# Replayed instruction orders for attention and the second convolution, a LayerNorm by pairs, and one chunk transposed on TensorE

## The chip, the cores and the metric

The kernel runs on one core of one Trainium2 chip. A core has five engines that work at the same time, each through its own instructions in program order: TensorE (PE: matrix products; its weight loads are listed apart as PEld), VectorE (DVE: elementwise work), ScalarE (ACT: activation functions and copies), GpSimd (POOL) and SyncE (SP, which here issues the DMA transfers). They meet through semaphores. An instruction that has to wait holds up everything behind it on its own engine, so the order in which a program hands work to an engine is part of its speed. Operands lie in SBUF (128 partitions) and matrix products land in PSUM, from where ACT or DVE copies them out ("evacuates" them).

The metric is the device time of one execution in microseconds (us); less is better. Besides, one execution was recorded by the hardware profiler; all rows below come from that one.

## What is computed

Four residual layers on x of shape (1, 2048, 512) in bfloat16, each behind a LayerNorm: a long convolution (an S4 layer by FFT), a sliding-window attention, and both once more with the same weights.

```python
def _A_ref(u, A_re, ..., Dskip):                 # convolution
    K = jnp.einsum("dn,dnl,dn->dl", Cc, P, dB).real        # P = exp(dt * A * l)
    ...
    Yf = Uf * Kf[None, :, :, :]                  # spectra of u and K, both padded to 2L
    y = irfft2(Yf)[..., :L]
    return y + u * Dskip

def _B_ref(x, wqkv, wo):                         # attention: 32 heads of 16, window 8, dilation 2
    ...
    idx = pos[:, None] - (jnp.arange(8) * 2)[None, :]
    ...
    logits = jnp.einsum("bhsd,bhswd->bhsw", q, kg) * scale
    attn = _softmax(jnp.where(mask, logits, -1e9))
    o = jnp.einsum("bhsw,bhswd->bhsd", attn, vg)
    return o.transpose(0, 2, 1, 3).reshape(B, S, D) @ wo

x = A_u
x = x + _A_ref(_layernorm(x), ...)
x = x + _B_ref(_layernorm(x), ...)
x = x + _A_ref(_layernorm(x), ...)
x = x + _B_ref(_layernorm(x), ...)
```

## The kernel before

The 2048 positions lie as 128 partitions by 16 token columns j; a group q is four of these columns (q = 0 is j 0 to 3, q = 3 is j 12 to 15). The residual x stays in SBUF as the tile `X` from start to end. The program has four stages, one after the other in the trace.

Stage 1 (`kernel_and_first_conv`, 0 to about 237 us) makes the spectrum of the convolution's kernel and runs the first convolution, in an order written out by hand. Stage 2 is attention 1 (`b_layer`, about 237 to 369 us), stage 3 convolution 2 (`a_layer`, 369 to 440 us), stage 4 attention 2 (`b_layer` again, 440 to 575 us).

An attention goes through these steps. `start(q)` (lines 1062 to 1098) normalises a group of `X` into `xn` (statistics on DVE, the root on ACT, line 160, scaling on DVE, lines 177 to 181) and transposes it into `xnT`: groups 0 and 3 on PE with a copy by ACT (`pt_x` line 1086, copy line 1089), groups 1 and 2 by DMA. `proj` (line 1110) makes queries and keys in 32 groups of four matmuls, each copied out by ACT into `qT` or `kT` (line 1115). The 32 heads are two family pairs, fp = 0 and 1, with a tile each: `kT_4078` and `kT_4079` are those of fp 0 and 1 in attention 1 and `kT_6218` and `kT_6219` in attention 2; `L_4082` and `L_4083` are the logits of fp 0 and 1 in attention 1. `values` (line 1130) makes v, copied out into `VX` (line 1135). `logits(fp, half)` multiplies q by shifted k on DVE, one product of 128x2048 for each of the 8 window offsets (line 1161; for the first half of fp 0 it is cut into 16 of 128x1024), and sums over the head's 16 elements on PE with a block matrix of ones (`Lp`, line 1171). ACT copies the sums (`LT`, line 1186), PE turns them (`pt_l`), ACT copies them into `L` (line 1197), and GpSimd masks the edge (line 1230). `softmax` (lines 1216 to 1243) runs on DVE with the exponential on ACT. `pv(fp, j0, nj)`, below "PV", multiplies `VX` by the weights on DVE, again a product for each offset (line 1254), and PE sums the 8 products with an identity matrix into `po` (lines 1270 and 1275). ACT copies `po` out (lines 1290 and 1292), a DMA transposes it into `oT`, and `out(qt)` (lines 1322 and 1324, `ps_o` and `ps_w`) adds the output projection to `X`, copied back by ACT (lines 1409, 1411 and 1452). PV comes in the pieces PV(0,0), PV(1,0) (columns j 0 to 7 of a family pair), PV(0,8), and PV(1,8), PV(1,12), PV(1,14) with 4, 2 and 2 columns; the products of these are 128x2048, 128x1024 and 128x512.

Behind attention 1 `normed` (lines 1413 to 1447) makes the LayerNorm for convolution 2 by groups: for q = 0 to 2 the mean from sums that ACT gathered (`ln_nm`, DVE, line 1437), four squares on ACT (line 1426), a root on ACT (line 168), scale on DVE, and the normalised columns on ACT (line 1430) or DVE into `U`. For q = 3 the statistics are DVE's (line 147).

Convolution 2 goes through four chunks dc of 128 channels. `s1` (line 804) takes one group of four columns of `U` through a transform on PE; ACT casts it into `Z` (line 808). `turn` transposes a chunk's `Z` into four tiles `zt` by SP's DMA queue (line 819). `s2` (lines 829 to 832) makes `xp`, ACT casts it to `xc` (line 836), `product` multiplies by the spectrum on DVE (`pa`, `pb`, lines 846 to 849), `inverse` transforms back on PE (`vp`), half of it copied by ACT and half by DVE (`VT`, line 868), and `final` adds to `X`.

What sets the order in stages 2 to 4 is a planner, the class `Plan`. The layer functions don't issue instructions at once: they register operations with `op` (engine, a cost in us from a table of estimates, the function that issues, its predecessors, and the PSUM and SBUF buffers that it takes and drops). `run` lists them: `ranks` gives each a priority, `place` simulates five engines and picks by rank, and 1200 random changes of the ranks are tried with a fixed seed; the best order is then issued. Each layer is planned by itself, as if all its inputs were there at its start; a pseudo operation `late` in `a_layer` holds back group 3 of `U` by 5 us.

## Time and profile before

| | us |
|---|---|
| median of 3 runs | 577.17 (574.05 to 578.47) |
| profiled execution, its own time | 576.7 |
| its span, first to last instruction | 574.9 |
| stage 2, attention 1 | about 237 to 369 |
| stage 3, convolution 2 | about 369 to 440 |
| stage 4, attention 2 | about 440 to 575 |

Around the span lie 1.8 us (576.7 - 574.9). A row of the timeline has a start, the time to its end, engine, line and operation, the output and the inputs, how often it repeats without a gap, and, in square brackets, how long the engine had been idle just before and on what the wait ended. Instructions of one engine overlap a little, so the time from start to start is often shorter than the duration. A row of windows has, for one stretch of the span, its length, and the busy time of each engine with its number of instructions, the clock that was granted to PE (1.00 is full), and what the DMA engines did.

### The profile page before, as it was taken

How to read it: one execution, taken by the hardware profiler on the slowest of the kernel's cores; microseconds unless marked ns; L12 is line 12 of the kernel's file. 1: busy time of each engine (PE TensorE's matmuls, PEld its weight loads, DVE VectorE, ACT ScalarE, POOL GpSimd, SP SyncE). 2: the span in 40 equal slices, each digit the busy share in tenths (PEclk: the TensorE clock that was granted, in tenths of full speed). 3: DMA queues.
4: the chain of work that ended last, by engine and by line, in shares of the span. 5: the costliest groups of instructions: out<-in, count | busy, mean ns of one | idle time of the engine just before them, and what ended most of it. 6: DMA issues, size and time to landing. Idle time of an engine off the chain costs nothing. (4 is left out here: it accounts for less than half of the span.)

```text
span 574.9 us, 11556 instructions
## 1 busy us (share of the span) xinstructions
PE 414.5 (72%) x4806; PEld 234.9 (41%) x4806; DVE 477.6 (83%) x803; ACT 340.2 (59%) x509; POOL 12.9 (2%) x62
## 2 busy tenths in 40 slices
PE   1102466777586589799995788678976999965997
PEld 0101333363363466443562334355654434632353
DVE  5999999999799886949789996508999378999980
ACT  4999655354455468675752147988763656622234
POOL 0000000000000004000000000000000000000000
PEclk9999987697798899999997699989996899987999
DMA  8200363646545465231033025439200310031142
GB/s 278 96 1 0 48 124 90 94 111 130 92 112 112 83 167 188 84 67 41 15 92 73 1 40 153 192 70 183 44 2 3 71 41 15 29 100 38 37 92 110
DMA packets 96031, 47.69 MB, mean 83 GB/s; under 512 B 85106, under 2 KB 91250, under 8 KB 94698
## 3 DMA queue, kind: packets, MB, share of 16 engines
q1 hardware_dynamic: 94394, 46.55, 34.1%
q8 instruction: 37, 0.61, 0.4%
q10 hardware_dynamic: 1584, 0.39, 0.3%
q14 instruction: 16, 0.13, 0.1%
HBM read 15.77 MB, written 8.13 MB: 42 GB/s over the span
## 5 line engine op out<-in xcount | busy, mean ns | idle before, releaser
L1161 DVE TENSOR_TENSOR prod<-qT,kT 128x2048 bf16<-128x2048 bf16 (+1 forms) x80 | 75.6, 1006 | 19.0 <-ACT kT L1115 10.8
L1254 DVE TENSOR_TENSOR prod<-VX,L 128x2048 bf16<-128x2048 bf16 (+2 forms) x96 | 76.9, 863 | 5.5 <-PE po L1275 2.0
L1110 PE MATMUL ps_qk<-xnT,wqk 128*128 128x512 bf16 x256 | 63.1, 385 | 2.2 <-ACT qT L1115 2.0
L1270 PE MATMUL po<-prod,sb_ident 128*128 128x512 bf16 x224 | 57.8, 409 | 7.6 <-DVE prod L1254 6.1
L212 PE MATMUL psA<-X,sb_F 128*128 128x128 bf16 x128 | 12.2, 238 | 43.3 <-ACT X L637 33.2
L212 PEld LDWEIGHTS <-sb_F 128*128 128x128 bf16 x256 | 17.5, 107 | 56.8 <-issue 56.1
L1171 PE MATMUL Lp<-prod,sb_bones 128*32 128x512 bf16 x256 | 29.6, 415 | 14.1 <-DVE prod L1161 14.0
L1270 PEld LDWEIGHTS <-sb_ident 128*128 128x128 bf16 x224 | 23.1, 104 | 39.2 <-issue 16.2
L1110 PEld LDWEIGHTS <-wqk 128*128 128x128 bf16 x256 | 23.0, 99 | 33.4 <-issue 12.7
L1290 ACT CAST ot<-po 128x1024 bf16<-128x1024 f32 x14 | 13.6, 1016 | 35.8 <-PE po L1270 34.2
L1130 PE MATMUL ps_v<-wv,xnT 128*128 128x256 bf16 x256 | 33.2, 278 | 1.1 <-ACT xnT L1089 0.8
L606 ACT CAST KTq<-psk 128x1024 bf16<-128x1024 f32 (+1 forms) x9 | 8.3, 917 | 43.1 <-PE psA L237 41.2
L596 PE MATMUL psk<-Ttab 128*32 128x64 bf16 x1024 | 20.9, 199 | 16.3 <-issue 16.3
L215 ACT CAST Z<-psA 128x1024 bf16<-128x1024 f32 (+1 forms) x32 | 28.8, 973 | 4.7 <-PE psA L212 4.6
L1324 PE MATMUL ps_o<-wo_t,oT 128*128 128x512 bf16 x112 | 29.1, 379 | 0.0
L578 DVE TENSOR_TENSOR Ttab<-Ttab,MPA 128x2048 bf16<-128x2048 bf16 (+2 forms) x20 | 27.7, 1431 | 0.0
L1130 PEld LDWEIGHTS <-xnT 128*128 128x128 bf16 x256 | 23.7, 99 | 9.5 <-issue 4.8
L1135 ACT CAST VX<-ps_v 128x512 bf16<-128x512 f32 x32 | 18.6, 588 | 14.8 <-PE ps_v L1130 14.8
L578 DVE TENSOR_TENSOR Y2tab<-Ttab,MPB 128x6144 bf16<-128x6144 bf16 (+1 forms) x13 | 27.2, 2119 | 0.0
L1115 ACT CAST kT<-ps_qk 128x512 bf16<-128x512 f32 x32 | 18.8, 587 | 13.6 <-PE ps_qk L1110 13.3
L1115 ACT CAST qT<-ps_qk 128x512 bf16<-128x512 f32 x32 | 18.7, 588 | 13.1 <-PE ps_qk L1110 12.9
L309 ACT CAST VT<-psA 128x512 bf16<-128x512 f32 x32 | 17.2, 589 | 13.3 <-PE psA L275 12.2
(200 smaller groups left out, 1014.9 us busy)
## 6 DMA issues: line engine op xcount, KB each, us to landing
X<-in_A_u_dram SPq DMA_DIRECT2D x8, 512.0 KB, 5.3
kt_scratch<-Kt SPq DMA_DIRECT2D x4, 1024.0 KB, 5.1
Kt<-kt_scratch SPq DMA_DIRECT2D x4, 1024.0 KB, 8.9
out_dram<-X SPq DMA_DIRECT2D x4, 512.0 KB, 2.6
k_scratch<-KTq SPq DMA_DIRECT2D x7, 256.0 KB, 2.4
KT<-k_scratch SPq DMA_DIRECT2D x7, 256.0 KB, 2.8
VX<-VX SPq DMA_DIRECT2D x4, 448.0 KB, 4.5
kT<-kT SPq DMA_DIRECT2D x8, 192.0 KB, 2.2
```

The lines of the kernel that those rows point to most:

```text
L212: nc.tensor.matmul(o, F1[:, j, r, :], rhs_j(j), start=True, stop=not dk)
L215: nc.scalar.copy(Z[:, 0:n // 8, :, jq * 32:(jq + 1) * 32].rearrange("p g r k -> p r g k"), ps[:, :, 0:n // 8, :])
L578: nc.vector.tensor_tensor(dst, src.to_broadcast([128, q, n, 2 * EYB]), mm.to_broadcast([128, q * n, EYB, 2]), ALU.mult)
L596: nc.tensor.matmul(o.rearrange("e (s i) -> e s i", s=2), xs, T[:, 1:3, h, m // 2, :, t], start=(m == 0), stop=False, skip_group_check=True)
L1110: nc.tensor.matmul(ps[:], wqk[:, ct, f0:f0 + 128], xnT[:, 4 * s:4 * s + 4, ct, :], start=(ct == 0), stop=(ct == 3))
L1115: nc.scalar.copy((qT, kT)[which][fp][:, f2, o:o + 512], box.pop(("qk", which, fp, f2, s))[:])
L1130: nc.tensor.matmul(ps[:, jj].rearrange("p t h d -> p (t h d)"), xnT[:, j + jj, ct, :], wv[:, ct, fp * 256:(fp + 1) * 256], start=(ct == 0) ...
L1161: nc.vector.tensor_tensor(pr[:, 0:n2], qT[fp][:, a:a + n2, j0 * 128:j0 * 128 + 1024], kT[fp][:, a:a + n2, c0:c0 + 1024], ALU.mult)
L1171: nc.tensor.matmul(Lp[r0:r0 + 32, w // 4, :], bones[:, w % 4, :], pr[:, f2 - a, hb * 512:(hb + 1) * 512], start=(n == 1), stop=(n == 4), s ...
L1254: nc.vector.tensor_tensor(p2[:, 0:nj].rearrange("p j t d h -> p (j t) d h"), VX[:, fp, NV + a:NV + a + nj].rearrange("p j (t d h) -> p (j ...
L1270: nc.tensor.matmul(po[:, c:c + 512], ident[:], p2[:, k + j:k + j + 2].rearrange("p j t d h -> p (j t d h)"), start=(n == 1), stop=(n == W))
L1324: nc.tensor.matmul(ps, box["oT"][:, ft // 2, j, ft % 2, :], wo_t[:, ft, :], start=False, stop=(ft == 3))
```

## The change

Stage 1 stays as it was. In stages 2 to 4 the change does five things.

1. `Plan` no longer plans. It replays `ORDERS`, three strings of operation numbers (attention 1, convolution 2, attention 2) that were searched beforehand; `outer` and `mark` are empty hooks that name links across the layers' borders (a group of `U`, a group of `X`). Everything that a layer issues, on all engines and the DMA queue, comes in the order of its string. The costs written in the `op` lines are no longer used for anything, so their edits issue nothing new.
2. The pseudo operation `late` is gone.
3. In chunks 0 and 1 of convolution 2 the group of the last four columns of `s1` is cut in two pairs: two evacuations of 128x2x16x16 take the place of one of 128x2x16x32.
4. Chunk 0's four transposes `zt` leave the DMA queue: 32 transposes on PE (a matmul against the identity, 128x128 each) into a PSUM tile `pt`, and four ACT copies of 128x1024.
5. The LayerNorm of group 3 behind attention 1 is done by pairs of columns: two roots and two scales of 128x2 take the place of one of 128x4.

```diff
-    def op(self, eng, us, fn, *after, take=None, drop=None, lag=None, boost=0.0):
...
-    def ranks(self):
...
-    def place(self, rank):
...
-    def run(self, tries):
...
+    turn = 0
+    def op(self, eng, us, fn, *after, **needs):
+        self.ops.append((fn, after))
+        return len(self.ops) - 1
+    def outer(self, tag):
+        return self.op("X", 0.0, None)
+    def mark(self, tag, *ops):
+        pass
+    def run(self):
+        order = [int(i) for i in ORDERS[Plan.turn].split()]
+        Plan.turn += 1
+        done = {i for i, (fn, after) in enumerate(self.ops) if fn is None}
...
+        for i in order:
+            fn, after = self.ops[i]
+            assert done.issuperset(after)
+            fn()
+            done.add(i)
+ORDERS = [
+    "1 13 2 3 14 5 4 7 8 6 15 10 16 9 18 19 17 11 21 126 23 78 127 33 20 24 44 79 25 34 28 61 29 45 35 31 37 63 38 62 "
...
 def a_layer
+PE_DC = (0,)
+ACT_VT = ()
-        def s1(dc, q, *after):
+        def s1(dc, j0, nj, *after):
...
         def turn(dc, c):
...
+            def mm():
+                pt = box["pt", c] = psA.tile([128, 8, 128], BF, name="pt", tag="psA")
+                for k in range(8):
+                    nc.tensor.transpose(pt[:, k, :], box["Z", dc][:, c * 4 + k // 2, k % 2, :], ident[:])
+            def evac():
+                zt = box["zt", dc, c] = zk.tile([128, 4, 2, 128], BF, name="zt", tag="zt")
+                nc.scalar.copy(zt[:].rearrange("q g r k -> q (g r k)"), box.pop(("pt", c))[:].rearrange("q k p -> q (k p)"))
+            if dc in PE_DC:
...
+                a = pl.op("P", 0.45, mm, *zdone[dc], take=key, drop=("Z", dc))
+                tdone[dc, c] = pl.op("A", 0.92, evac, a, take=("zt", dc, c), drop=key)
+                return
...
-        late = pl.op("S", 0.0, lambda: None, lag=5.0)
         for dc in range(4):
-            for q in range(4):
-                prev = s1(dc, q, *([late] if q == 3 else []), *([] if prev is None else [prev]))
+            prev = []
+            for j0, nj in ((0, 4), (4, 4), (8, 4), (12, 2), (14, 2)) if dc < 2 else ((0, 4), (4, 4), (8, 4), (12, 4)):
+                prev = [s1(dc, j0, nj, pl.outer(("u", j0 + nj - 1)), *prev)]
...
 def normed
                 if q == 3:
-                    o = [pl.op("V", 0.69, lambda j=j: stats(j, j + 1), after[j - j0]) for j in range(j0, j1)]
-                    o = pl.op("A", 0.25, lambda: ln.root(j0, j1), *o)
-                    pl.op("V", 1.75, norms, o)
+                    for k in (j0, j0 + 2):
+                        o = [pl.op("V", 0.69, lambda j=j: stats(j, j + 1), after[j - j0]) for j in (k, k + 1)]
+                        o = pl.op("A", 0.25, lambda k=k: ln.root(k, k + 2), *o)
+                        o = pl.op("V", 0.25, lambda k=k: ln.scale(k, k + 2), o)
+                        for j in (k, k + 1):
+                            pl.mark(("u", j), pl.op("V", 0.32, lambda j=j: ln.norm(U[:, j, :], X[:, j, :], j), o))
                     return
```

How the strings move instructions is told best by the rows that each engine is handed. Three places follow, each before and then after the change. The line numbers of the changed kernel differ: its logits products are line 1123 (before 1161), its PV products 1216 (before 1254), its `ln_nm` 1398 (before 1437), its evacuation of `po` 1252 and 1254, its `kT` and `qT` copies 1077 (before 1115), its roots 161 and 169, its `xc` 849 (before 836).

The first place is on DVE in attention 1, where the weights of fp 1's first half come out of the softmax (reciprocal and multiplication into `L_4083`). Before, the eight products of the second half's logits of fp 1 (`qT_4081`, `kT_4079`) stand together ahead of it, and PV(1,0) starts behind:

```order
L1161 TENSOR_TENSOR prod<-qT_4081,kT_4079 128x2048 x8
L1216 TENSOR_TENSOR sm_s_4912<-L_4083 128x512
L1218 TENSOR_TENSOR sm_s_4914<-sm_s_4912 128x256
L1220 TENSOR_TENSOR sm_s_4916<-sm_s_4914 128x128
L1239 RECIPROCAL sm_rdb<-sm_s_4916 128x128
L1240 TENSOR_TENSOR L_4083<-L_4083,sm_rdb 128x1024
L1254 TENSOR_TENSOR prod_4937<-VX,L_4083 128x2048
```

After, PV(1,0) starts at once: one of these logits products stands behind its first product, and the others follow behind its eighth (the numbers after the names count buffers):

```order
L1202 TENSOR_TENSOR L_4083<-L_4083,sm_rdb 128x1024
L1216 TENSOR_TENSOR prod_4875<-VX,L_4083 128x2048
L1123 TENSOR_TENSOR prod<-qT_4081,kT_4079 128x2048
L1216 TENSOR_TENSOR prod_4887<-VX,L_4083 128x2048
L1216 TENSOR_TENSOR prod_4893<-VX,L_4083 128x2048
L1216 TENSOR_TENSOR prod_4899<-VX,L_4083 128x2048
L1216 TENSOR_TENSOR prod_4905<-VX,L_4083 128x2048
L1216 TENSOR_TENSOR prod_4911<-VX,L_4083 128x2048
L1216 TENSOR_TENSOR prod_4917<-VX,L_4083 128x2048
L1216 TENSOR_TENSOR prod_4923<-VX,L_4083 128x2048
L1216 TENSOR_TENSOR prod_4929<-VX,L_4082 128x2048
L1123 TENSOR_TENSOR prod<-qT_4081,kT_4079 128x2048 x6
```

All eight logits products have moved from ahead of PV(1,0): one is behind its first product, six behind its last and one product of PV(0,8) (`L_4082`), and the eighth two rows further down. Further down in the same layer, the first `ln_nm` (line 1437, now 1398) stood behind eight PV products of 128x1024 and four of 128x512; now it stands behind three of 128x1024.

The second place is on ACT at the border from attention 1 to convolution 2. Before, nine casts of `Z` stand together ahead of these rows, and the last three of the twelve are followed by the first `xc`:

```order
L808 CAST Z<-ps_s_5518 128x2x16x32
L808 CAST Z<-ps_s_5508 128x2x16x32
L808 CAST Z<-ps_s_5496 128x2x16x32
L836 CAST xc<-xp 128x1024
L808 CAST Z<-ps_s_5542 128x2x16x32
L836 CAST xc<-xp 128x1024
L808 CAST Z<-ps_s_5567 128x2x16x32
L836 CAST xc<-xp 128x1024 x2
L808 CAST Z<-ps_s_5585 128x2x16x32
```

After, the rows from the fifth `Z` on are these; four full casts stand ahead:

```order
L808 CAST Z<-ps_s_5428 128x2x16x32
L808 CAST Z<-ps_s_5449 128x2x16x32
L808 CAST Z<-ps_s_5476 128x2x16x16
L808 CAST Z<-ps_s_5471 128x2x16x16
L808 CAST Z<-ps_s_5482 128x2x16x32
L829 COPY zt<-pt 128x1024
L808 CAST Z<-ps_s_5492 128x2x16x16
L829 COPY zt<-pt 128x1024 x2
L849 CAST xc<-xp 128x1024 x2
L829 COPY zt<-pt 128x1024
L849 CAST xc<-xp 128x1024
```

Ahead of the first `xc` there stand now seven full casts of `Z`, three half ones and three of the four copies of `zt`, where twelve full casts stood; the other casts follow between the `xc`.

The third place is on ACT at the start of attention 2, where the copies of `kT` and `qT` follow PE's projection groups. Before (`kT_6218` and `qT_6220` are fp 0's, `kT_6219` fp 1's):

```order
L160 ACTIVATE ln_den_b_4027<-ln_mv_b_4026,eps 128x4 x2
L1089 COPY xnT<-pt_x 128x1024 x2
L1135 CAST VX<-ps_v 128x512
L1115 CAST kT_6218<-ps_qk 128x512
L160 ACTIVATE ln_den_b_4027<-ln_mv_b_4026,eps 128x4
L1115 CAST qT_6220<-ps_qk 128x512
L1115 CAST kT_6219<-ps_qk 128x512
L160 ACTIVATE ln_den_b_4027<-ln_mv_b_4026,eps 128x4
L1115 CAST qT_6220<-ps_qk 128x512
L1115 CAST kT_6219<-ps_qk 128x512
```

After (`kT_6261` and `qT_6263` are fp 0's, `kT_6262` fp 1's):

```order
L161 ACTIVATE ln_den_b_4027<-ln_mv_b_4026,eps 128x4 x2
L1051 COPY xnT<-pt_x 128x1024 x2
L1097 CAST VX<-ps_v 128x512
L161 ACTIVATE ln_den_b_4027<-ln_mv_b_4026,eps 128x4
L1077 CAST kT_6261<-ps_qk 128x512
L161 ACTIVATE ln_den_b_4027<-ln_mv_b_4026,eps 128x4
L1077 CAST qT_6263<-ps_qk 128x512 x2
L1077 CAST kT_6262<-ps_qk 128x512
L1051 COPY xnT<-pt_x 128x1024
L1077 CAST kT_6261<-ps_qk 128x512
L1051 COPY xnT<-pt_x 128x1024
```

The third and fourth roots of the LayerNorm stood behind one and three copies and now stand ahead of and behind the first one; the third and fourth `xnT` copies come after four and five copies of `kT` and `qT`, where they came after seven and eight. On PE the projection groups and turns stand in the same order as these copies: ahead of the last sum of logits(0,0) there are 17 groups instead of 22, and in attention 1, in the same way, 18 instead of 22.

On SP's DMA queue the rows keep their order but for two things: 12 instead of 16 transposes `zt`, and the seventh and last `oT` transpose of attention 2 stands behind two stores of `out_dram` instead of one. GpSimd's rows are the same.

185 lines of the change are left out of this document (43 added, 142 removed), and 34 rows, old and new, of the table ORDERS.

## Prediction

> **What bounds the kernel now.** I read the span first, then windows by stage, then DVE's timeline, and last who DVE waits for.
>
> ```profile
> core 0: 574.9 us, clock 0.923
> PE 414.5 (72%) x4806; PEld 234.9 (41%) x4806; DVE 477.6 (83%) x803; ACT 340.2 (59%) x509; POOL 12.9 (2%) x62
> core 0: us, PE busy (x) PEld busy (x) DVE busy (x) ACT busy (x) POOL busy (x), PEclk, DMA share, GB/s
> 237.00:369.00 132.00, 113.56 (x728) 54.42 (x726) 106.45 (x192) 75.10 (x138) 2.39 (x20) 0.94 0.26 74
> 349.00:369.00 20.00, 16.73 (x123) 9.09 (x121) 8.72 (x28) 19.21 (x49) 0.00 (x0) 1.00 0.62 224
> 369.00:387.00 18.00, 10.03 (x111) 8.08 (x111) 4.41 (x15) 17.07 (x23) 0.00 (x0) 0.91 0.23 44
> 387.25:440.50 53.25, 43.61 (x354) 29.21 (x351) 50.25 (x108) 36.66 (x52) 0.00 (x0) 0.94 0.37 65
> 452.90:489.00 36.10, 35.09 (x220) 14.65 (x219) 23.51 (x34) 23.34 (x36) 0.88 (x7) 1.00 0.11 31
> 488.90:562.00 73.10, 60.65 (x387) 30.82 (x386) 69.36 (x91) 26.41 (x37) 1.51 (x13) 0.91 0.26 58
> 510.00:528.00 18.00, 10.75 (x56) 4.44 (x56) 17.77 (x19) 3.95 (x4) 0.31 (x3) 0.79 0.16 30
> ```
>
> The median of the runs is 577.17; the profiled execution took 576.7, 1.8 more than its span, so my sum works on the span and adds 1.8. DVE has the most work, and in two long stretches nothing else binds: 50.25 busy of 53.25 (3.00 idle) and 69.36 of 73.10 (3.74 idle). Elsewhere it waits. From 349 to 387 it works 8.72 + 4.41 of 38 us while ACT works 19.21 + 17.07: ACT binds there. From 452.9 to 489 DVE works 23.51 of 36.10 while PE works 35.09: PE binds there. These two holes hold 24.9 and 12.6 us of idle DVE; an order can earn nothing but idle time, since the change removes no work from DVE.
>
> ```profile
> 257.81 8.53 DVE L1161 TENSOR_TENSOR prod<-qT,kT 128x1024 bf16<-128x1024 bf16 x14 [2.49 <-ACT kT L1115]
> 276.17 0.42 DVE L1216 TENSOR_TENSOR sm_m<-L 128x512 bf16<-128x512 bf16 x1 [2.57 <-POOL L L1230]
> 295.76 4.63 DVE L1254 TENSOR_TENSOR prod<-VX,L 128x2048 bf16<-128x2048 bf16 x4 [1.58 <-ACT VX L1135]
> 309.20 9.16 DVE L1161 TENSOR_TENSOR prod<-qT,kT 128x2048 bf16<-128x2048 bf16 x8
> 343.87 6.25 DVE L1254 TENSOR_TENSOR prod<-VX,L 128x1024 bf16<-128x1024 bf16 x12
> 350.04 0.16 DVE L1437 TENSOR_SCALAR ln_nm<-ln_sum 128x4 f32<-128x4 f32 x1
> 387.25 0.69 DVE L846 TENSOR_TENSOR pa<-xc,Kt 128x1024 bf16<-128x1024 bf16 x1 [13.24 <-ACT xc L836]
> 457.81 0.69 DVE L1161 TENSOR_TENSOR prod<-qT,kT 128x1024 bf16<-128x1024 bf16 x1 [4.95 <-ACT kT L1115]
> 488.98 3.50 DVE L1161 TENSOR_TENSOR prod<-qT,kT 128x2048 bf16<-128x2048 bf16 x3 [1.81 <-ACT qT L1115]
> 549.60 2.50 DVE L1254 TENSOR_TENSOR prod<-VX,L 128x1024 bf16<-128x1024 bf16 x4
> 560.41 1.43 DVE L1254 TENSOR_TENSOR prod<-VX,L 128x512 bf16<-128x512 bf16 x4 [0.45 <-PE po L1275]
> 350.64 0.72 ACT L1426 ACTIVATE U<-X,ln_nm 128x512 bf16<-128x512 bf16 x1
> 374.11 0.99 ACT L808 CAST Z<-ps_s 128x1024 bf16<-128x1024 f32 x1
> 377.01 9.29 ACT L808 CAST Z<-ps_s 128x1024 bf16<-128x1024 f32 x10 [0.69 <-PE ps_s L804]
> 386.12 1.09 ACT L836 CAST xc<-xp 128x1024 bf16<-128x1024 f32 x1
> 370.19 0.30 ACT L168 ACTIVATE ln_den_a<-ln_sq,eps 128x4 bf16<-128x4 f32 x1
> ```
>
> Read the rows from 343.87 to 387.25 as one chain. DVE reaches `ln_nm` at 350.04; ACT's first square follows at 350.64; ACT then works without a pause worth naming through squares, `X` copies and norms to its first `Z` at 374.11 (23.5 us later), casts twelve `Z`, and its `xc` at 386.12 lets DVE's first product of convolution 2 go at 387.25 (13.1 us later).
>
> **The change part by part.** The sum goes along that chain.
>
> *Start of attention 1.* PE is the bound:
>
> ```profile
> 243.00:280.00 37.00, 37.00 (x226) 15.39 (x223) 26.41 (x57) 24.01 (x40) 0.88 (x7) 1.00 0.21 51
> 243.43 7.07 PE L1110 MATMUL ps_qk<-xnT,wqk 128*128 128x512 bf16 x32
> 268.08 1.02 ACT L1186 CAST LT<-Lp 128x1024 bf16<-128x1024 f32 x1
> 472.81 1.01 ACT L1186 CAST LT<-Lp 128x1024 bf16<-128x1024 f32 x1
> ```
>
> A projection group takes 7.07/8, some 0.88 us. Four fewer stand ahead of the sums, 3.5 us; of these I give back 1.0, since the fourth turn of `xnT` now comes early and its input may not be ready, so `LT` comes at about 265.6 instead of 268.08 (-2.5). The waits behind it, 2.57 and 1.58 in the rows above, are the same chain seen from DVE, and the values and fp 1's projections that filled PE ahead of it go behind. Walking DVE's new order with these durations, I get the first product of PV(0,0) earlier by 4.3 than 295.76 less its own equal work. Bounds: 2.5 (nothing of the later waits goes) to 2.49 + 2.57 + 1.58 = 6.6 (all three rows). I take 4.3, about midway, as the walk has it.
>
> *Logits behind PV(1,0).* The order of products doesn't change DVE's sum, but what the chain waits for. Eight logits products of 9.16 together leave the place ahead of PV(1,0). So columns 0 to 7 reach PE's output projection about 4.3 + 8 = 12 us earlier, and ACT has `X` in time for squares. The first `ln_nm` stood behind eight products of 128x1024 and four of 128x512 (6.25 in the row at 343.87) and stands now behind three of 128x1024 (2.50/4 each by the row at 549.60, 1.9): 4.4 less. With 4.3 that makes 8.7, the square at about 342. DVE's other products follow `ln_nm` on its queue; if `X` is late, all of them wait. My walk has `X` ready 0.9 us ahead.
>
> *ACT up to `Z`.* The same squares, norms and copies, 23.5 us, and one root more, 0.30 by the last row above; the second pair's scale runs on DVE in its hole and costs nothing as long as DVE idles there. First `Z` at 374.11 - 8.7 + 0.3 = 365.7, or -8.4.
>
> *From `Z` to the first product.* Ahead of the first `xc` there stood twelve casts. There stand now seven full and three half ones and three copies of `zt`:
>
> ```profile
> 251.01 1.02 ACT L1089 COPY xnT<-pt_x 128x1024 bf16<-128x1024 bf16 x1
> 366.01 0.58 ACT L1411 CAST X<-ps_o 128x512 bf16<-128x512 f32 x1
> zt<-Z SPq DMA_TRANSPOSE x16, 3.3
> ```
>
> A full cast is 9.29/10, 0.93; a half one is bounded by 0.46 (half of that) and 0.58 (a cast of 128x512 out of PSUM), I take 0.5; a `zt` copy has no row, its nearest is the 1.02 of the same shape in `xnT`, some 0.93 when queued. 7 x 0.93 + 3 x 0.5 + 3 x 0.93 = 10.8, against 374.11 to 386.12 = 12.0. So -1.2 if nothing waits, and -9.6 at the first product: 377.6. The DMA path that goes (3.3 to land, behind a chunk's last cast) was partly covered by the next chunk's casts; the eight PE transposes that take its place are covered by a cast of chunk 2. What the copies cost: 4 x 0.93 = 3.7 us of ACT where ACT binds, 2.8 of it in the sum above, the fourth behind the second `xc`. SP loses four issues; its rows behind are the same and none is late. GpSimd gets the same rows.
>
> *Rest of convolution 2.* DVE-bound, same products: 0. ACT's extra half casts and fourth copy, about 1.2, lie beside 36.66 busy of 53.25.
>
> *Attention 2.* DVE's idle 12.59 from 452.9 to 489 is what can go. PE puts 17 groups ahead of the last sum where 22 stood: 5 x 0.88 = 4.4, less 0.7 for sums that bunch up, so `LT` is 3.7 earlier than 472.81 (relative to the stage). The first product's key copy moves from PE's tenth group to the seventh (3 x 0.88 = 2.6 of the 4.95 wait). The new order also puts six products of 128x2048 ahead of the softmax's return where three stood, and all eight of fp 1's first half right behind it, so that the waits there (1.81 at 488.98 is the last) are filled. Of the 12.59, the first wait keeps 4.95 - 2.6 = 2.3, and DVE waits some 4 more while PE's groups release the 16 short products one by one (the 2.49 at 257.81 is such a wait in attention 1); the rest, 6.3, goes. Ends: 3.7 (`LT` alone) to 12.6 (all the idle). I take 6.3, nearer to the low end, as `LT` sets it. What was moved behind, 128x512 value copies and `ps_v`, goes into the hole that PE has from 510 to 528 (10.75 busy of 18, first fence). The tail from DVE's last product (560.41 + 1.43 = 561.84) to the last store is PE's and ACT's, with the same `po` and `ps_o` rows up to these two of the chain of waits, so 0:
>
> ```profile
> 569.96 0.88 PE ps_o L1324 x4
> 570.86 0.58 ACT X L1452
> ```
>
> *New waits.* No row prices them. A dense order meets small waits: the two dense stretches carried 3.00 and 3.74. Ends 0 and 6.7; the walk already carries some, I add 2.5.
>
> Sum: 574.9 - 9.6 - 6.3 + 2.5 = 561.5 in span, 563.3 in time; I say 563. With all bounds at their good end it would be some 552, with all at the bad end (2.5 instead of 4.3, 3.7 instead of 6.3, 6.7 instead of 2.5, -1.2 lost) about 573.
>
> [...] PE ran its 16 turns twice, at different rates:
>
> ```profile
> 240.62 1.36 PE L1086 MATMUL pt_x<-sb_ident,xn 128*128 128x128 bf16 x16 [1.68 <-DVE xn L181]
> 442.43 1.89 PE L1086 MATMUL pt_x<-sb_ident,xn 128*128 128x128 bf16 x16 [3.08 <-DVE xn L181]
> ```
>
> After 1.68 idle they took 1.36, after 3.08 idle 1.89: PE is slower after the longer pause, and the stretch from 510 to 528, with 7.25 of 18 idle, has the lowest granted clock quoted, 0.79. The change's 32 turns cost 2.7 to 3.8 by these rows, in a stretch where PE is busy 10.03 of 18, so they hide. [...]
>
> **Rivals.** *A, ACT binds the border.* If `X` or `U` comes late and ACT's chain can't start earlier, only -1.2 is earned there: 574.9 - 1.2 - 6.3 + 0 + 1.8 = 569. For it: ACT is busy 19.21 of 20. Against: what it waits for is DVE's place for `ln_nm`, which moved. 0.13. *B, attention 2 earns nothing*, since a `VX` shift (DMA) or a copy is late: 569.6. For it: this stage's PE is 35.09 busy of 36.10 and gets no less work. 0.08. *C, slow turns.* PE comes out of 32 turns at a low clock, and the 16 `s2` matmuls behind them, 0.22 each by the chain's row of four, take twice that: 3.5 us, 567. For it: 442.43's row, 1.4 times 240.62's. Against: DVE needs a chunk's `xc` one by one, and the later ones have slack. 0.04. *D, the change doesn't do what it says*: the order was made against estimates, and DVE's queue now has `ln_nm` among its products; with `X` 8 us late there and B besides, it ends within 1% of before, 571.4 to 582.9. 0.12. *E, slower by PE's clock.* PE's two dense stretches, 37 us at 1.00 and 36 at 1.00, lose their clock as PE gets denser. At the 0.79 of 510 to 528 they'd be 73 x 0.27 = 19.5 longer: 583. It decides from 0.84 down (14 us, break-even with 577.17); slower by over 1%, above 582.9, begins just under 0.79. Against: in this trace the clock is full where PE is dense and low where it idles. 0.05.
>
> **How the numbers follow.** The forecast has 0.58. About 1% is what a measurement of this kernel can tell from no change; 577.17 less 1% is 571.4. A, B, C and the forecast lie below it: 0.83, less 0.01 for their upper ends, 0.82 faster. D and that 0.01 make 0.13 within 1%, and E 0.05 slower. The range 555 to 573 takes in the forecast's ends, A, B, C and D's edge; it leaves out E and most of D above (0.14) and 0.04 below.
>
> **What would show it.** Right: DVE's first product of convolution 2 near 378, its 13.24 wait much smaller, first square near 342, first `Z` near 366; in attention 2 the 4.95 wait halved and an `LT` about 13 us earlier than 472.81; PE busier and at a higher clock where 510 to 528 was. Wrong: DVE waiting at `ln_nm` for an `X` sum (A, D), waits on `VX` or `qT` in attention 2 (B), `xp` at half rate behind the turns (C), a clock under 0.85 where PE is dense (E).

## The result and the profile after

The changed kernel takes 560.76 us (median of 4 runs, 559.12 to 562.7); the kernel before, run beside it, takes 576.6 (574.05 to 578.47). The ratio is 0.973, with a 95% interval from 0.9678 to 0.9781: faster by 2.7%. The profiled execution took 562.7, the slowest of the four, with a span of 560.9. The first lines of its page:

```profile
core 0: 560.9 us, clock 0.935
PE 412.3 (74%) x4838; PEld 236.1 (42%) x4838; DVE 477.0 (85%) x805; ACT 343.8 (61%) x516; POOL 12.9 (2%) x62
```

The engines' work hardly differs: DVE 477.0 against 477.6, ACT 3.6 more, PE 2.2 less. What changed is when they wait. To see where, cut both traces at the same events: DVE's first statistics of attention 1, ACT's first square, ACT's first `Z`, DVE's first product of convolution 2, DVE's first `BATCH_NORM_AGGREGATE` of attention 2, and DVE's end. These are the windows of the kernel before between these events (the fifth begins where the fourth ends):

```profile
core 0: us, PE busy (x) PEld busy (x) DVE busy (x) ACT busy (x) POOL busy (x), PEclk, DMA share, GB/s
237.44:350.64 113.20, 98.02 (x611) 45.91 (x610) 98.92 (x169) 56.39 (x90) 2.39 (x20) 0.92 0.20 47
350.64:374.11 23.47, 15.86 (x123) 8.86 (x122) 11.93 (x38) 23.38 (x59) 0.00 (x0) 0.99 0.53 191
374.11:387.25 13.14, 9.51 (x104) 7.66 (x104) 0.00 (x1) 12.21 (x14) 0.00 (x0) 0.89 0.33 64
387.25:439.57 52.32, 43.61 (x354) 29.21 (x351) 49.32 (x100) 35.96 (x51) 0.00 (x0) 0.93 0.37 66
439.57:561.84 122.27, 105.64 (x652) 51.01 (x653) 103.14 (x177) 56.42 (x85) 2.39 (x20) 0.92 0.22 50
```

And these are the same five windows of the changed kernel:

```profile
239.60:345.44 105.84, 95.86 (x604) 45.10 (x603) 94.80 (x161) 57.42 (x93) 2.39 (x20) 0.97 0.20 48
345.44:368.85 23.41, 19.19 (x153) 10.69 (x152) 14.38 (x43) 23.32 (x55) 0.00 (x0) 1.00 0.55 202
368.85:380.80 11.95, 9.21 (x72) 6.77 (x72) 1.92 (x8) 11.74 (x16) 0.00 (x0) 0.71 0.00 0
380.80:431.36 50.56, 42.44 (x394) 29.74 (x391) 49.41 (x100) 39.52 (x56) 0.00 (x0) 0.98 0.37 64
431.36:547.69 116.33, 106.09 (x664) 50.52 (x665) 102.28 (x177) 57.26 (x86) 2.39 (x20) 0.92 0.24 57
```

Read the first number behind each window, its length. The five differ by -7.36, -0.06, -1.19, -1.76 and -5.94, together -16.31. Against that, stage 1, which the change doesn't touch, ended 2.16 later in this execution (239.60 against 237.44), and the stretch behind DVE's end took 0.15 more: 574.9 - 16.31 + 2.16 + 0.15 = 560.9. In the first window, DVE's busy time falls by 4.12 (98.92 to 94.80: work that now stands behind the square) and its idle time by 3.24 (14.28 to 11.04).

Rows of the timeline of the changed kernel that answer to those of before:

```profile
280.77 0.42 DVE L1178 TENSOR_TENSOR sm_s<-L 128x512 bf16<-128x512 bf16 x1 [2.18 <-ACT L L1205]
345.24 0.16 DVE L1398 TENSOR_SCALAR ln_nm<-ln_sum 128x4 f32<-128x4 f32 x1
345.44 0.72 ACT L1384 ACTIVATE U<-X,ln_nm 128x512 bf16<-128x512 bf16 x1 [0.74 <-DVE ln_nm L1398]
368.85 7.45 ACT L808 CAST Z<-ps_s 128x1024 bf16<-128x1024 f32 x9
380.80 0.69 DVE L859 TENSOR_TENSOR pa<-xc,Kt 128x1024 bf16<-128x1024 bf16 x1 [9.96 <-ACT xc L849]
446.65 0.69 DVE L1123 TENSOR_TENSOR prod<-qT,kT 128x1024 bf16<-128x1024 bf16 x1 [3.68 <-ACT kT L1077]
459.68 1.01 ACT L1148 CAST LT<-Lp 128x1024 bf16<-128x1024 f32 x1 [0.17 <-PE Lp L1133]
472.73 0.42 DVE L1178 TENSOR_TENSOR sm_s<-L 128x512 bf16<-128x512 bf16 x1 [2.38 <-ACT L L1205]
```

`ln_nm` waits for nothing, and ACT waits only 0.74 for it. The wait at the first product of convolution 2 fell from 13.24 to 9.96, the one at attention 2's first product from 4.95 to 3.68 (not to half, as the prediction had it). Two waits are new in size: DVE now stands 2.18 and 2.38 for the exponential of the first softmax, where it had stood some 0.5 at that row in attention 1.

### The profile page after: what moved, and what is told of

The parts are those of the page before. It is cut to its first block, busy times and chain, and to the rows that moved or that the text cites. A ratio compares the mean times of both kernels' runs of the same rounds, so it can differ in the third digit from the quotient of the medians.

```text
span 560.9 us, 11633 instructions
## 1 busy us (share of the span) xinstructions
PE 412.3 (74%) x4838; PEld 236.1 (42%) x4838; DVE 477.0 (85%) x805; ACT 343.8 (61%) x516; POOL 12.9 (2%) x62
## 4 chain that ended last, share of the span: by engine, by line
PE 38%; DVE 35%; ACT 14%; DMA 6%; issue 6%; SPq 1%; DVEq 0%; ACTq 0%
PE ps_qk L1072 8%; PE po L1232 5%; PE ps_v L1092 4%; DVE prod L1216 3%; PE Lp L1133 3%; DVE Ttab L579 3%; DMA zt<-Z 2%; PE ps_o L1286 2%; DVE ln_st_b L148 2%; DVE Ttab L547 2%; DVE Y2tab L579 2%; DVE prod L1123 2%; ACT Z L808 2%; DVE tb L544 2%; DVE Ttab L543 2%
## 5 line engine op out<-in xcount | busy, mean ns | idle before, releaser
L1232 PE MATMUL po<-prod,sb_ident 128*128 128x512 bf16 x224 | 59.0, 411 | 10.4 <-DVE prod L1216 9.5
L213 PEld LDWEIGHTS <-sb_F 128*128 128x128 bf16 x256 | 19.0, 112 | 59.0 <-issue 58.1
L597 PE MATMUL psk<-Ttab 128*32 128x64 bf16 x1024 | 22.5, 206 | 13.9 <-issue 13.9
L1133 PE MATMUL Lp<-prod,sb_bones 128*32 128x512 bf16 x256 | 28.1, 394 | 1.0 <-DVE prod L1123 0.8
```

What stands on the lines that cost most here:

```text
L213: nc.tensor.matmul(o, F1[:, j, r, :], rhs_j(j), start=True, stop=not dk)
L597: nc.tensor.matmul(o.rearrange("e (s i) -> e s i", s=2), xs, T[:, 1:3, h, m // 2, :, t], start=(m == 0), stop=False, skip_group_check=True)
L1133: nc.tensor.matmul(Lp[r0:r0 + 32, w // 4, :], bones[:, w % 4, :], pr[:, f2 - a, hb * 512:(hb + 1) * 512], start=(n == 1), stop=(n == 4), s ...
L1232: nc.tensor.matmul(po[:, c:c + 512], ident[:], p2[:, k + j:k + j + 2].rearrange("p j t d h -> p (j t d h)"), start=(n == 1), stop=(n == W))
```

## The experiments

All ratios are to the kernel before on the same chip. "To the first `Z`" counts from DVE's first statistics of attention 1, so that stage 1's differences between executions are left out (129.25 in the changed kernel, 136.67 before).

**Each stage alone.** Theory: the gains of the three stages are local and add up. Rivals: one carries all, or one gives back what another earns. First the changed kernel with the old order in attention 2:

```diff
@@ ORDERS[2] (attention 2)
-    "1 13 2 3 14 5 4 6 8 7 15 10 18 9 16 19 17 11 21 126 23 61
+    "1 13 2 3 14 5 6 4 7 8 15 10 19 9 17 18 11 126 16 21 23 44
...
```

> The changed kernel with attention 2 put back to the order of before (attention 1 and convolution 2 as changed). Theory, the gains of the layers add up and attention 2's order is worth about 5.8 us (its stretch from the last statistics of the LayerNorm to the end was 5.8 shorter in the changed kernel's trace): 566.6 us. Rival, the whole gain hangs on the first border and attention 2 is bound by its work: 561. Rival, attention 2's new order carries more than its stretch shows: over 570.

Then the kernel before with only attention 2's new order; the LayerNorm by four columns is that of the edit further below:

```diff
-PE_DC = (0,)
+PE_DC = ()
-            for j0, nj in ((0, 4), (4, 4), (8, 4), (12, 2), (14, 2)) if dc < 2 else ((0, 4), (4, 4), (8, 4), (12, 4)):
+            for j0, nj in ((0, 4), (4, 4), (8, 4), (12, 2), (14, 2)) if dc < 0 else ((0, 4), (4, 4), (8, 4), (12, 4)):
@@ ORDERS[0], ORDERS[1]: the orders of before
-    "1 13 2 3 14 5 4 7 8 6 15 10 16 9 18 19
+    "1 13 2 3 14 4 5 6 8 7 15 9 10 16 17 11
...
-    "1 4 56 59 2 5 107 60 7 8 57 108 10 13
+    "1 4 2 7 49 5 52 50 55 56 8 53 10 97
...
```

> The kernel before with attention 2 alone in its new order. Theory, additive: 576.6 less 5.8, 570.8 us, and DVE's first product of convolution 2 stays at about 387. Rival, attention 2's order only pays behind the new convolution 2: 576.

Third, only attention 1 with its LayerNorm by pairs (`s1` uncut as above):

```diff
-PE_DC = (0,)
+PE_DC = ()
@@ ORDERS[1], ORDERS[2]: the orders of before
...
```

> The kernel before with attention 1 in its new order and its last LayerNorm by pairs; convolution 2 and attention 2 as before. Theory: the first cast of Z comes 7.4 us earlier and the rest follows it, 569.2 us. Rival, convolution 2's old order, planned as if its last group came late, takes nothing from an earlier start: 575 to 576. Rival in between: 572.

Fourth, only convolution 2, with the LayerNorm by four columns as in the second run:

```diff
@@ ORDERS[0], ORDERS[2]: the orders of before
...
```

> The kernel before with convolution 2 alone changed (new order, chunk 0 on TensorE, split groups); attention 1 with its LayerNorm by one group, attention 2 as before. Theory: 1.2 from the first cast of Z to the first product and 1.8 inside the layer, 573.6 us. Rival, the four copies of zt cost what the order earns, 576.6. Rival, this part is what frees the border: under 570.

Measured: the changed kernel with the old attention 2 has 0.984 [0.9808, 0.9872]; attention 2 alone 0.9886 [0.9864, 0.9908]; attention 1 alone 0.990 [0.9866, 0.9935]; convolution 2 alone 0.9955 [0.9925, 0.9984]. The three single ones save 1.14 + 1.0 + 0.45 = 2.6%, the whole 2.7%: the gains add up, and attention 2 and attention 1 carry most. One piece does not stand alone. From the first `Z` to the first product takes 13.14 before and 11.95 after, but 14.51 with attention 1 alone and 13.50 with convolution 2 alone. These are ACT's casts in the kernel with attention 1 alone:

```profile
370.73 1.01 ACT L808 CAST Z<-ps_s 128x1024 bf16<-128x1024 f32 x1 [1.61 <-PE ps_s L804]
372.44 8.34 ACT L808 CAST Z<-ps_s 128x1024 bf16<-128x1024 f32 x9 [0.69 <-PE ps_s L804]
```

The old order of convolution 2, started earlier, waits 2.30 in two places for PE's `ps_s` (0.90 in the kernel before). The new order of convolution 2 behind the old attention 1 is no shorter than before. So the 1.19 needs the new order of attention 1 too. The LayerNorm by pairs, which came with it, is not what matters: done by four columns again (a run further down), the stretch takes 12.29.

**The transposes of chunk 0 back on the DMA queue.**

```diff
-PE_DC = (0,)
+PE_DC = ()
@@ ORDERS[1]: the operations renumbered, their order adapted
...
```

> The changed kernel with chunk 0's four transposes back on the DMA queue, issued where the first TensorE turns stood; all other rows keep their order. Theory: the first zt lands 3.3 us behind the chunk's last cast, about 1.3 later than the copy by ACT was done, but three ACT copies (2.8 us) no longer stand ahead of the first xc; from the first cast of Z to DVE's first product 12.5 us instead of 11.95, and the total within 1 us of the changed kernel. Rival, TensorE's turns are what makes the border short: 15 us or more and a total 3 us up. Rival, the copies cost more than the DMA's latency: 11 us or less.

Measured: 0.9704 [0.9609, 0.9799]; 12.86 from the first `Z` to the first product instead of 11.95. ACT's row at the first `xc`:

```profile
380.95 1.01 ACT L849 CAST xc<-xp 128x1024 bf16<-128x1024 f32 x1 [3.87 <-PE xp L845]
```

And the DMA view of these 15 us, with the median time from issue to landing last:

```profile
zt<-Z SPq DMA_TRANSPOSE x4, 3.1
```

ACT has fewer casts ahead of the first `xc`, but then stands 3.87 while the DMA takes 3.1 to land. PE's turns are worth 0.91 at that point, a small part of the whole, and the interval can't tell the total from the changed kernel's.

**The logits of fp 1's second half back ahead of PV(1,0).** In the string, the operations 253 to 268 (products and sums of these logits, and what follows them) move up as a block:

```diff
@@ ORDERS[0]
-    222 224 223 272 253 273 225 276 254 274
+    222 224 223 253 254 259 260 261 262 265 266 263 264 255 256 257 258 267 268 272 273 225 276 274
```

> The changed kernel with the eight logits products of fp 1's second half and their sums put back ahead of PV(1,0). Theory: PV(1,0) ends 8 us later, its columns of X come that much later, DVE stops at the first ln_nm for some 7 us, and the first cast of Z and all behind it come 7 us later: 568 us. Rival, DVE's products are the same in either order and ACT or PE catch up: at most 2 us.

Measured: 0.9758 [0.9644, 0.9872]; `ln_nm` and the first `Z` come 4.57 later, between the two expectations. DVE's timeline shows where it lies:

```profile
318.50 14.84 DVE L1217 TENSOR_TENSOR prod<-VX,L 128x2048 bf16<-128x2048 bf16 x13
336.89 2.36 DVE L1217 TENSOR_TENSOR prod<-VX,L 128x2048 bf16<-128x2048 bf16 x2 [3.55 <-PE po L1233]
339.74 0.43 DVE L1179 TENSOR_TENSOR sm_m<-L 128x512 bf16<-128x512 bf16 x1 [0.49 <-POOL L L1193]
342.80 0.43 DVE L1179 TENSOR_TENSOR sm_s<-L 128x512 bf16<-128x512 bf16 x1 [0.18 <-ACT L L1206]
347.93 0.17 DVE L1399 TENSOR_SCALAR ln_nm<-ln_sum 128x4 f32<-128x4 f32 x1 [0.34 <-ACT X L1373]
```

The four waits sum to 4.56, the whole loss; none of them is among the changed kernel's waits of that stretch. Put first, the logits leave 15 PV products with nothing between them, and DVE runs into PE's `po`. So the move earns by filling holes on DVE. The `X` that comes earlier, which the prediction named, is a second path beside it: ACT's last sum for these columns ends 105.1 behind the first statistics in the changed kernel and 110.2 here, 5.1 later, and `ln_nm` shows only 0.34 of that because DVE itself came late. Both moved together, and this run can't tell what either alone would have cost.

**The first `ln_nm` five products later, behind eight.**

```diff
@@ ORDERS[0]
-    319 376 393 320 380 324 378 329 322 394 321 326 379 323 325 395 330 377
+    319 393 320 324 329 322 394 321 326 323 325 395 330 376 380 378 379 377
```

> The changed kernel with the first ln_nm and its squares put behind eight instead of three PV products of 128x1024 (five more, 3.05 us), one copy of X ahead of the squares. Theory, the chain from ln_nm over ACT's squares to the first cast of Z is the bound: the cast comes 2.3 to 3 us later, total up by as much. Rival, ACT has slack there, or PE's output projections are the bound: under 1 us.

Measured: 0.9691 [0.9612, 0.9769]; the first `Z` 3.37 later, a little more than the theory's 2.3 to 3. The chain `ln_nm`, squares, `Z` does bind. The profiled span was nonetheless 560.7, since 2.41 came back in attention 2 (the last section tells why) and stage 1 ended 1.58 sooner in this execution. The total alone would have refuted a mechanism that the segment shows.

**The second quarter's norms on DVE instead of ACT.**

```diff
-                    if q == 2:
+                    if q in (1, 2):
```

> The changed kernel with the four normalisations of group 1 behind attention 1 on DVE instead of ACT, in the same place of the order (an attempt to go below the changed kernel). Theory, ACT binds from the first square to the first xc while DVE idles: ACT loses 4 x 0.72 = 2.9 us, and the first cast of Z comes 2 to 2.9 us earlier. Rival, PE's output projections are the bound there already: under 1 us. Rival, DVE's statistics of group 3 stand behind the added rows and are late: no gain or a loss.

Measured: 0.965 [0.9508, 0.9791]; the first `Z` 1.29 earlier, less than expected. A window from the middle of that stretch:

```profile
360.00:366.00 6.00, 5.95 (x31) 2.77 (x30) 2.81 (x9) 4.92 (x13) 0.00 (x0) 1.00 1.01 427
```

And ACT's first wait in it, from the timeline:

```profile
361.31 0.60 ACT L1373 ACTIVATE X<-ps_o 128x512 bf16<-128x512 f32 x1 [0.49 <-PE ps_o L1287]
```

ACT has air (4.92 of 6.00) and PE has none (5.95): freed of four norms, ACT waits for the output projections here. In the windows beside it ACT is full (5.97 of 6.00 from 354 to 360, 3.97 of 4.00 from 366 to 370). So ACT binds a part of the stretch and PE another, and of the 2.9 that ACT no longer does, 1.29 reach the first `Z`.

**The first exponentials two places earlier on ACT**, to remove the new waits of 2.18 and 2.38:

```diff
@@ ORDERS[0]
-    107 203 196 108 84 109 101 85 187 204 116
+    107 203 204 196 108 84 109 101 85 187 116
@@ ORDERS[2]
-    90 203 192 91 88 92 124 89 195 204 84
+    90 203 204 192 91 88 92 124 89 195 84
```

> The changed kernel with the first exponential of both attentions (and the table load ahead of it) two places earlier on ACT, ahead of two copies of k and q. It tests why the start of both attentions gained less than was forecast: DVE waits 2.2 to 2.4 us for this exponential. Theory, PE's projections bound this stretch: the wait shrinks to about 0.8 but PE stands longer for the copies, and the first PV product comes at the same time within 0.5 us. Rival, the exponential's place is what costs: each attention's first PV product comes 1.5 us earlier, 3 us in all.

Measured: 0.9695 [0.9632, 0.9758]; the first PV product no earlier (54.06 behind the first statistics, 53.85 in the changed kernel). Rows of DVE and ACT:

```profile
279.40 0.43 DVE L1179 TENSOR_TENSOR sm_s<-L 128x512 bf16<-128x512 bf16 x1 [0.21 <-ACT L L1206]
280.95 0.58 ACT L1078 CAST qT<-ps_qk 128x512 bf16<-128x512 f32 x1 [0.62 <-PE ps_qk L1073]
285.15 9.18 DVE L1124 TENSOR_TENSOR prod<-qT,kT 128x2048 bf16<-128x2048 bf16 x8 [2.96 <-ACT kT L1078]
```

The wait at the exponential is gone, and the next one, for the `kT` copies of fp 1, takes its place: 2.18 + 0.79 before the edit, 0.21 + 2.96 after it. In attention 2 it is the same: 2.38 + 0.79 became 0.21 + 2.96, and the first PV product comes 38.76 behind the first logits product in both kernels. So the place of the exponential was not the bound. That PE's projection groups are is argued, not shown: ACT's copies wait for PE's `ps_qk` (the middle row), and PE is busy 48.40 of the 50 us from 250 to 300 in the changed kernel. In both orders PE itself stands some 1.5 us (1.55 here, 1.45 in the changed kernel) while ACT loads the table (1.28) and computes the exponential (1.06).

**The last LayerNorm by four columns again.**

```diff
-                    for k in (j0, j0 + 2):
...
+                    o = [pl.op("V", 0.69, lambda j=j: stats(j, j + 1), after[j - j0]) for j in range(j0, j1)]
+                    o = pl.op("A", 0.25, lambda: ln.root(j0, j1), *o)
+                    pl.op("V", 1.75, norms, o)
```

> The changed kernel with the last LayerNorm group done by four columns with one root and one scale, at the place of the second pair's. Theory, the pairs let two columns' normalisations run about 1 us earlier, but the first casts of Z wait for other groups: from the start of stage 2 to the first cast of Z 129.0 to 129.3 us as in the changed kernel (one root of 0.3 less), from there to the first product 12.0 to 12.5 instead of 11.95. Rival, the pairs matter: 13 us or more. Rival, they cost: 11.6 or less.

Measured: 0.970 [0.9635, 0.9764]; the first product of convolution 2 comes 141.67 behind the first statistics, against 141.20. With 0.3 of that already present at the start of the attention, the pairs are worth some 0.2 and can't be told from nothing, as the theory had it.

**Three edits together**: the norms on DVE, the front of convolution 2 reordered so that DVE makes two casts of `Z` and its first product comes sooner, and 24 matmuls whose result nobody reads in PE's pause ahead of attention 2, which are work beside the computation.

```diff
+DVE_Z = ((1, 0), (1, 4))
+WARM = 24
...
+                eng = nc.vector.tensor_copy if (dc, j0) in DVE_Z else nc.scalar.copy
...
+        def warm():
+            w = psA.tile([128, 2, 512], F32, name="warm", tag="psA")
+            for k in range(WARM):
+                nc.tensor.matmul(w[:, k % 2, :], ident[:], Kt[0][:, 0, 0, :], start=True, stop=True)
+        pl.op("P", 5.2, warm)
...
@@ ORDERS[1]: a new order of convolution 2
...
```

> The changed kernel with three edits, each read from a stretch of its own. One, group 1's normalisations on DVE, as in the run before. Two, at the start of convolution 2 the casts of chunk 1's first two groups go to DVE, and chunk 0's casts, turns and products stand ahead of those of chunks 1 and 2. Three, 24 matmuls of 128x512 that nothing reads run on PE in its 6.1 us pause ahead of attention 2. Theory: first cast of Z 1.3 us earlier; from there to the first product 10.0 us instead of 11.95, as 2.8 us of other casts no longer stand ahead; the clock stays full over the border, and the stretch from the last LayerNorm statistics to attention 2's first product is 13.9 us, the shortest that was seen, instead of 15.3. Together some 4.5 us below the changed kernel: 556 to 557 on its scale of before at 576.6. Rival, the DVE casts or the order starve chunk 1, and convolution 2 gives back inside what its start gains: 559. Rival, the idle matmuls delay attention 2 or leave the clock as it was: 14.5 us or more in that stretch.

Measured: 559.4 (4 runs), ratio 0.9663 [0.9609, 0.9718], not the 556 to 557 expected. The first product did come 2.3 sooner behind the first `Z` (9.66 instead of 11.95), but the rest of convolution 2 took 54.61 instead of 50.56. DVE's rows:

```profile
378.19 0.69 DVE L862 TENSOR_TENSOR pa<-xc,Kt 128x1024 bf16<-128x1024 bf16 x1 [5.42 <-ACT xc L852]
389.02 0.69 DVE L884 CAST VT<-vp 128x512 bf16<-128x512 f32 x1 [4.75 <-ACT VT L884]
```

Behind the third product stands a `VT` cast on DVE's queue that waits for ACT's `VT` cast, and ACT's stands behind the fourth `xc` and four casts of `Z` and comes at 388.40: 4.75 of standing for 2.3 gained. The edit moved the front and not what stands behind it.

**The same without the front**: norms on DVE and the unread matmuls.

> The changed kernel with two edits: the second quarter's norms on DVE, and 24 matmuls whose result is not read (they are work beside the computation) at the end of convolution 2, where PE pauses ahead of attention 2. The front of convolution 2 stays as in the changed kernel, since its gain there was returned at a VT cast of 4.75 us. Theory (the gains are local and add up): first Z 1.3 us earlier than in the changed kernel as in the run with the norms alone; 50.5 from the first product of convolution 2 to the second block's first BATCH_NORM_AGGREGATE; then the first turn of attention 2 at full clock (16 turns in about 1.07 instead of 1.9) and 13.2 from that aggregate to the first product (15.29 in the profile of the changed kernel, 14.52 with the norms alone); span 557 to 558, median 557.5. Rival (the clock is full early in most executions anyway, so that the unread matmuls earn nothing in the median): as the norms alone, 559.2 or above.

Measured: 558.08 (6 runs, 556.09 to 560.54), ratio 0.9656 [0.9625, 0.9686], the lowest median here. Most segments came as the theory had them: 22.12 from the first square to the first `Z`, as with the norms alone (23.41 in the changed kernel), 50.51 inside convolution 2, and 13.20 from the first aggregate of attention 2 to its first product (15.29 in the changed kernel). From the first `Z` to the first product it took 12.23 instead of 11.95. Its interval and the changed kernel's overlap (0.9678 to 0.9686), so that it beats the changed kernel is likely by the medians and supported by the segments, not settled by the totals. Nor do the totals show that the unread matmuls earn anything: the norms alone have 0.965 in their 2 runs, with a wide interval, so the rival is refuted in the segment alone.

## Why the prediction was right, step by step

The forecast was 563.0, the measurement 560.76, inside the range of 555 to 573. In span: 561.5 forecast, 560.9 found. That near hit is in part luck: errors of opposite sign cancel, one of them is stage 1's 2.16, and the profiled execution was the slowest of the four (at the median the span is some 559.0, which is 560.76 - 1.8). The terms tell more than the total.

- *Start of attention 1, -4.3; `ln_nm`, -4.4.* The second was right: 4.12 of DVE's work moved behind the square. The first is mis-sized: 3.24 of idle time went, between the ends 2.5 and 6.6. `LT` did come 2.5 earlier (28.10 behind the first statistics instead of 30.64), and the waits of 2.57 and 1.58 behind it did go. But the walk had no new waits in their place, and there were some: 1.41 for `qT`, 2.18 at the exponential, 0.79 for `kT`. The run with earlier exponentials showed that the 2.18 only covers the next wait.
- *`X` ready 0.9 ahead of `ln_nm`.* Right, with less to spare: the row of `ln_nm` shows no wait, and ACT's last sum ends at 344.70, 0.5 ahead. Rival A, an `X` or `U` that comes too late for an earlier start, did not occur, and delaying `ln_nm` moved the first `Z` by 3.37.
- *Square to first `Z`, +0.3.* It came out as -0.06.
- *First `Z` to first product, -1.2.* Found -1.19. The run with the DMA transposes gave 0.91 of it back, and the single-stage runs show that it needs attention 1's new order besides.
- *Rest of convolution 2, 0.* This step failed, found -1.76. "DVE-bound, same products" overlooked one row. The two rows of the kernel before are what ACT did ahead of its second `xc`, and DVE's second product:

```profile
389.29 1.01 ACT L808 CAST Z<-ps_s 128x1024 bf16<-128x1024 f32 x1 [2.07 <-DMA zt<-Z]
391.25 0.69 DVE L846 TENSOR_TENSOR pa<-xc,Kt 128x1024 bf16<-128x1024 bf16 x1 [1.91 <-ACT xc L836]
```

  ACT stood 2.07 at a `Z` cast until a `zt` transpose had landed, the second `xc` stood behind it, and DVE lost 1.91. The new order issues the first two `xc` together, and the wait is gone. It also stays gone with the transposes on DMA (50.62 there), so it is the order and not the path that removed it. It was within the 3.00 idle that the prediction quoted and read as the small waits of any dense order.
- *Attention 2, -6.3.* Found -5.94 to DVE's end. Its parts were sized low: the first product came 2.95 earlier within the stage (2.6 forecast), `LT` 4.92 (3.7 forecast). It gains as much alone (1.14%). These are sizes of one execution each, and the clock moves them (last section): over the four profiled kernels with the old order of attention 2, DVE's end comes 119.9 to 122.3 behind the first aggregate, over the eight with the new one and no unread matmuls 113.9 to 116.5, by the means 6.6 earlier. No run here varied the moves inside attention 2 singly, so which of them earns what is argued from the waits.
- *New waits, +2.5.* Mis-sized: none beyond those that are in the terms above. The two waits at the exponential are new, but they took the place of others.
- *Tail, 0.* Found +0.15. Stage 1's +2.16 was no term at all; it is a difference between two executions of the same instructions.

Against the span of 561.5 the errors, in the order above and with work and idle time of the start together, are +1.3, -0.4 (the square to `Z`), 0.0, -1.8, +0.4, -2.5, +0.15 and +2.16: together -0.6.

*Rival C, slow turns.* The turns did run slowly, but what follows did not. PE's rows in the changed kernel:

```profile
375.45 2.74 PE L825 MATMUL pt<-sb_ident,Z 128*128 128x128 bf16 x24 [0.39 <-ACT Z L808]
377.98 0.63 PE L842 MATMUL xp<-zt,sb_C 128*128 128x512 bf16 x1
378.73 0.38 PE L844 MATMUL xp<-zt,sb_C 128*128 128x512 bf16 x1
```

Windows there, from the moment at which the clock fell and each 3.41 us long (the last section tells why), with the granted clock third from the end:

```profile
371.78:375.19 3.41, 2.59 (x20) 1.93 (x19) 0.00 (x0) 3.41 (x5) 0.00 (x0) 0.50 0.00 0
375.19:378.61 3.42, 3.16 (x26) 2.83 (x27) 0.00 (x0) 3.21 (x5) 0.00 (x0) 0.50 0.00 0
378.61:382.02 3.41, 3.40 (x30) 1.98 (x28) 1.22 (x2) 3.41 (x5) 0.00 (x0) 1.00 0.00 0
```

Twenty-four turns at a clock of 0.50, then only two `xp` matmuls below full speed: the clock had risen 3.16 us after the turns began. 2.59 us of `s1` matmuls in the first window brought no rise, and the rise came behind the second, in which 2.74 of the 3.16 busy us are turns and only 0.42 are other matmuls. So two matmuls were slow (0.63 at 377.98, 0.48 at 378.41, and 0.38 from 378.73 on) and not sixteen, and the 3.5 us of this rival were not lost.

*Rivals B, D and E* did not occur: attention 2 earned 5.94, the order did what it says, and the granted clock in attention 1 went up (0.92 to 0.97 in the first window) as PE got denser (98.02 of 113.20 us busy, then 95.86 of 105.84), not down.

## To carry to other kernels

Price a change of order by the idle time of the engine that binds, stage by stage, and give every wait in a "dense" stretch a row of its own: the 1.91 that looked like friction was one queue position. Removing a visible wait earns nothing where the next dependence is due at the same time, as with the exponential here, and a gain at a stage's front is kept only if the rows behind it move along on every engine, as the 4.75 at `VT` showed. Where totals scatter by 2 to 4 us, judge an edit by segments between equal events; the late `ln_nm` cost 3.4 us and its total showed nothing.

## What the runs showed of the hardware that was not expected

PE pauses for 6.1 us ahead of attention 2 and restarts at half clock (0.50). How long it then takes to reach full clock differs between executions of the same instructions. PE's rows at this place, first in the changed kernel, then in the run with the earlier exponentials, whose PE instructions there are the same:

```profile
433.89 1.89 PE L1048 MATMUL pt_x<-sb_ident,xn 128*128 128x128 bf16 x16 [6.10 <-DVE xn L182]
436.08 1.89 PE L1092 MATMUL ps_v<-wv,xnT 128*128 128x256 bf16 x8 [0.31 <-ACT xnT L1051]
437.76 4.75 PE L1072 MATMUL ps_qk<-xnT,wqk 128*128 128x512 bf16 x16
```

```profile
434.67 1.89 PE L1049 MATMUL pt_x<-sb_ident,xn 128*128 128x128 bf16 x16 [6.10 <-DVE xn L182]
436.86 1.57 PE L1093 MATMUL ps_v<-wv,xnT 128*128 128x256 bf16 x8 [0.31 <-ACT xnT L1052]
438.27 3.62 PE L1073 MATMUL ps_qk<-xnT,wqk 128*128 128x512 bf16 x16
```

The 16 projection matmuls take 4.75 in the one and 3.62 in the other, 3.99 and 4.37 in two further runs: full clock came between about 3.2 and 6.4 us after the restart. In the eight profiled kernels with the new order of attention 2 and no unread matmuls (the pause is 6.1 in seven of them, and 2.63 where convolution 2 has its old order), the first product of attention 2 comes 13.84 to 15.43 behind the first aggregate, and DVE's end 113.9 to 116.5. It is what made the run with the late `ln_nm` look harmless.

The traces also show where the executions part. In the traces of both kernels, the moments within the span at which the granted clock changes lie whole multiples of 3.413 us apart (in the changed kernel 371.79, 378.61, 429.81 and 440.05 lie 2, 15 and 3 times that apart); where this grid lies differs from execution to execution (the kernel before has a change at 373.55, 1.76 from 371.79). The two windows of this grid around the restart, first in the changed kernel, then in the run with the earlier exponentials:

```profile
433.22:436.64 3.42, 2.44 (x19) 2.06 (x20) 3.35 (x13) 1.62 (x2) 0.00 (x0) 0.50 0.00 0
436.64:440.05 3.41, 3.41 (x13) 1.66 (x11) 2.79 (x18) 1.42 (x4) 0.00 (x0) 0.50 0.80 154
```

```profile
434.56:437.97 3.41, 3.00 (x22) 2.43 (x23) 3.34 (x17) 1.93 (x2) 0.00 (x0) 0.50 0.00 0
437.97:441.39 3.42, 3.42 (x19) 1.74 (x18) 3.12 (x18) 2.48 (x6) 0.00 (x0) 1.00 0.82 158
```

In the changed kernel the restart at 433.89 falls 0.67 into a window; PE is busy for 2.44 of it, and the clock rises only behind the next window, 6.2 us after the restart. In the other run the restart falls 0.11 into a window; PE is busy for 3.00 of it, and the clock rises at its end, 3.3 us after the restart. Two more runs agree: 2.71 busy brought no rise (chunk 0's transposes on the DMA queue), 2.92 did (the LayerNorm by four columns).

The unread matmuls test this: they shorten the pause from 6.10 to 0.92. Rows of the kernel with norms on DVE and these matmuls:

```profile
425.99 5.34 PE L927 MATMUL warm<-Kt,sb_ident 128*128 128x512 bf16 x24
432.25 1.07 PE L1056 MATMUL pt_x<-sb_ident,xn 128*128 128x128 bf16 x16 [0.92 <-DVE xn L183]
434.94 3.64 PE L1080 MATMUL ps_qk<-xnT,wqk 128*128 128x512 bf16 x16
442.92 0.69 DVE L1131 TENSOR_TENSOR prod<-qT,kT 128x1024 bf16<-128x1024 bf16 x1 [2.85 <-ACT kT L1085]
```

The turns take 1.07 instead of 1.89 and the projections run at full speed from the first (granted clock 1.00 from 427 to 442). Two executions with the matmuls have the same 13.20 to the first product, where those without them scatter. No run here varied the pause in steps, and the traces show no single busy time from which the clock rises: elsewhere in the changed kernel it rose behind windows with 2.49 us (98.72 to 102.13) and 2.71 us busy (153.34 to 156.75), and did not behind one with 2.80 (313.77 to 317.18).
